# Two query/key buffers, first values in the weight ring, three weight loads from ScalarE's queue, a one-join decode and a new order, in a fused attention and two-MLP kernel

## Chip, cores and metric

The kernel runs on one core of a Trainium2 chip. The metric is the device time of one execution in microseconds. Before the change it was 1083.62 us, the median of three runs (1083.09 to 1084.38). The profiled execution took 1084.31 us, and the stretch that its trace covers, from the first to the last instruction, is 1082.5 us.

## What is computed

Chunked attention with memory slots, then a two-layer MLP with a rational activation, then a gated MLP. q, k and v are float32; all weights are float64.

```python
# attention: 4 batches, 8 heads, 768 positions, head dimension 64, chunks of 32 queries
for c in range(24):
    k_ctx = k[:, :, max(0, 32*c - 16) : min(768, 32*c + 40)]        # v_ctx the same
    k_full = concat([mem_k, k_ctx]); v_full = concat([mem_v, v_ctx]) # 8 memory rows first
    a = softmax(q_c @ k_full.T / 8)
    out[:, :, 32*c : 32*c + 32] = a @ v_full
x = attn_out as 3072 tokens x 512
h = x @ w_in                                        # 512 -> 2048
g = (a0 + a1*h + a2*h**2 + a3*h**3) / (1 + |b0|*|h| + |b1|*h**2 + 1e-6)
x = g @ w_out                                       # 2048 -> 512
y = (((x @ w1) * (x @ w2)) @ w3) @ w_out2           # 512 -> 1024 twice, gate, 1024 -> 1024 -> 512
```

## The kernel before

**Precision and decode.** A matmul with float32 accuracy is made of three passes (`mm3`, line 281; the `pe.matmul` is line 284): high part times high part, high times low, low times high. Each weight chunk, 128 x 512 values of float64, comes from HBM as 512 KB of raw 32-bit words into a ring of four tiles (`raw`). `decode` turns it into a high and a low part in seven steps: the load; `scale` (ScalarE, L242), which brings the upper word into float32's exponent range; `low` (L248 on ScalarE, L250 on VectorE), which takes the top three bits of the lower word; two joins (VectorE, L255 and L257); `high_part` (ScalarE, L265); `low_part` (L268, GpSimd, or VectorE for some chunks). `MODES` names, for each of the 32 chunks of the first MLP, where scaled values lie (PSUM bank "h" or "att", or in place) and which engine takes `low` (ScalarE for capital letters).

**Attention.** A unit u is 128 queries of all heads; there are 24, six in each batch. Its steps: `load_qk` (L299, four transfers of 64x4x160 words, and L302, four small ones for the memory keys, where the buffer is new to the batch), `load_v` (L308 to L311), scores `sc` on TensorE (L326), maximum, difference and sum on VectorE (L336, L339, L347), exponential on ScalarE (L343), normalization `e` (L357), transposition `at` on TensorE (L362), copies `aT` (ScalarE L371, VectorE L373), values `xo` on TensorE (L380), and the split into `xr`, high on ScalarE (L388), low on VectorE (L390). There is one buffer each for q/k, v and e.

**First MLP.** Tokens are in 8 blocks of 384, three units each; the 2048 hidden columns in 16 chunks f. Step n of `SEQ` is a block and an f: `gemm1` (h, 12 matmuls), the rational function (`rat_*`, ScalarE, VectorE, GpSimd), `gemm2` (acc, 12 matmuls), which trails by four steps. The first two blocks are interleaved by halves: block 0 with f 0 to 7 (here h0 to h7), block 1 with f 0 to 7 (h8 to h15), then f 8 to 15 of either (h16 to h31). So h8 needs units 3 to 5, and h16 the first weight chunk beyond the eighth. All 32 chunks are decoded beside these steps.

**Second MLP.** `ab` (L284) are the two gate inputs, `w3o` folds w3 and w_out2 into one matrix, `pr` are products of a seven-product scheme over half blocks.

**What sets the order.** Every operation is a `step` with a nominal time, the engines that can take it, what it follows, and the ring slots it takes. `order()` deals the steps out to the engines by earliest start and nominal time; the program is then written out in that order, and each engine runs its list strictly in that order. SP issues all transfers of this part from one list. Numbers such as `T0`, `UP`, `R`, `SI` or `DO` are only nominal times.

Of the kernel before, what the change touches and what calls it, by code (L numbers as in the profile page):

```python
# [41 lines left out]
SIGN = -2 ** 31  # L42

# [13 lines left out]
def attention_rational_mlp_gated_mlp(  # L57
# [18 lines left out]
    QBUF, VBUF, EBUF = 1, 1, 1  # L76
# [152 lines left out]
    def decode(t, src, dst, *ready, take=(), early=(), LOW=None, tag=None, byte=False):  # L229
# [5 lines left out]
        def load():  # L235
            r.append(raw("w64"))
            sp.dma_start(out=r[0], in_=src.bitcast(I32).rearrange("p (k t) -> p k t", t=2))
# [21 lines left out]

        def value():  # L260
            return b[0] if inps else r[0][:, :, 0].bitcast(F32)
# [31 lines left out]
    def load_qk(u):  # L293
        b, j = divmod(u, UPS)
        t = q_t[u % QBUF]
        for g in range(2):
            r, h = slice(g * D, (g + 1) * D), slice(g * HG, (g + 1) * HG)
            for s in range(NS):
                sp.dma_start(out=t[r, :, s, :QB + KW], in_=qkT[b, j * NS + s, :, h])  # L299
            if j < QBUF:  # L300
                for s in range(NS):
                    sp.dma_start(out=t[r, :, s, QB + KW:], in_=qkT[b, 0, :, h, QB:QB + NMEM])  # L302

    def load_v(u):
        b, j = divmod(u, UPS)
        t = v_t[u % VBUF]
        for s in range(NS):
            sp.dma_start(out=t[:CK, s], in_=vW[b, j * NS + s, :CK])  # L308
            sp.dma_start(out=t[CK:P - NMEM, s], in_=vW[b, j * NS + s, W1:])
            if j < VBUF:  # L310
                sp.dma_start(out=t[P - NMEM:, s], in_=vW[b, 0, :NMEM])  # L311
# [63 lines left out]
    def v_pe(u, tag):  # L375
        xo = st[u] = bank(tag, "xo")
        for s in range(NS):
            for h in range(H):
                i, g = divmod(h, 2)
                pe.matmul(xo[g * D:(g + 1) * D, i * UQ + s * QB:i * UQ + (s + 1) * QB], lhsT=v_t[u % VBUF][:, s, h],  # L380
                          rhs=aT[:, s, g * (H // 2) + i].rearrange("p c q -> p (c q)"), start=True, stop=True)
# [196 lines left out]
    H0 = 1.272  # L578


    MODES = "KNnhahkKkNNNNNNNHNmmHAaMAaaaANAn"
    HOW = {"n": (None, LOWA), "h": ("h", LOWA), "a": ("att", LOWA), "m": (None, two("d", 0, .602)), "k": ("h", two("d", 0, .64))}
# [14 lines left out]
    T0 = -8.139; UP = -3.210; A0 = -2.685; AS = 1.874  # L597
# [3 lines left out]
    SLACK = 0.4  # L601
    NORM = "pd"
# [3 lines left out]
    LEAD = 4  # L606
    LEAD2 = 9
    A1 = -2.388
    A2 = -2.780

    def loads(u, t):
        lq[u] = step(t - 3, {"dma": 2.65}, lambda: load_qk(u), *old(first, lq[u - 1]), take=("q",))
        lv[u] = step(t - 2, {"dma": 2.0}, lambda: load_v(u), *old(lv[u - 1]), take=("v",))
        return lq[u]
# [38 lines left out]
    R = (-1.427,0.216,0.543,0.964,1.286,6.975,-0.116,0.555,0.902,0.154,1.541,1.594,-0.009,-1.683)  # L653
    DI = -2.973
    DO = -3.438
    WI, WO = {}, {}
    SI = 0.893
    SO = 0.844
    DJ = -3.554
    DP = -3.457  # L660
    SJ = 0.944
# [40 lines left out]
    for k, (t, o, f) in enumerate(chunks):  # L702
        (WO if o else WI)[f] = decode(t, *((w_out[f], wB[:, f]) if o else (w_in[f], wA_slot(f))), tag=HOW[MODES[k].lower()][0],
                                      byte=MODES[k].isupper(), LOW=HOW[MODES[k].lower()][1])
# [20 lines left out]
    TG, TO, TM = 1.727, 0.363, -0.182  # L725
    TB = n1 + LAG - 0.1
    XB = 0
# [62 lines left out]
    for i in range(NF2):  # L790
        W3[i] = [decode(tO[i] + 0.5 * g + D3, w3T[i, :, g], w3_dst(i, g), sec, take=("w3",), early=[sec] if i < 2 else [O[i - 2]], LOW=LOWT[g % len(LOWT)], tag=TAGT[g % len(TAGT)], byte=BYTT[g % len(BYTT)]) for g in range(2)]
# [10 lines left out]
    LG2 = 3  # L802
# [13 lines left out]
    XT, XS, SL, SH, GT, OT = -6.742, -5.180, -1.545, 0.934, -2.825, -0.532  # L816
# [345 lines left out]
```

## Time and profile before

| | |
|---|---|
| time, median of three | 1083.62 us |
| profiled execution | 1084.31 us |
| its span | 1082.5 us |
| TensorE busy | 1040.6 us, 96% of the span |
| VectorE, ScalarE, GpSimd busy | 759.1, 671.6, 483.9 us |
| mean granted TensorE clock | 0.984 of full speed |

Busy time of TensorE contains slow stretches: the same twelve matmuls of 128x384 take about 2.1 us at full clock and about 4.1 us at half. So an idle gap can cost twice, once as a gap and once as the slow matmuls behind it. The program is a pipeline whose start has to be filled; the page's slices show TensorE at 90% or more from the fifth of the 40 slices on.

### The profile page before, as it was taken

The numbers are of one execution on the slowest core, as the hardware profiler recorded it, in microseconds if no ns is written. First come the engines' busy times: TensorE is split into PE (matmuls) and PEld (weight loads), VectorE is DVE, ScalarE is ACT, GpSimd is POOL, SyncE is SP. The second block draws the span as 40 slices with busy tenths as digits, with TensorE's granted clock in tenths as the row PEclk, the third lists the DMA queues.
The fourth block names the chain that finished last, engine by engine and source line by source line (L and its number), as shares of the span: only waits on it lengthen the run. The fifth ranks groups of instructions, "written<-read, shape, count | busy, mean of one in ns | idle before, by whom it ended". The sixth has DMA issues, their size and how long they took to land.

```text
span 1082.5 us, 20045 instructions
## 1 busy us (share of the span) xinstructions
PE 1040.6 (96%) x7632; PEld 985.5 (91%) x7632; DVE 759.1 (70%) x1326; ACT 671.6 (62%) x1290; POOL 483.9 (45%) x438
## 2 busy tenths in 40 slices
PE   2697999999999999999999999999999999999998
PEld 2587999999999999999999999988899999998997
DVE  4889999787777777777779987875485563663330
ACT  3687998677777777777779996644233252343222
POOL 1255675444434444444446776723133263344233
PEclk9688999999999999999999999999999999999999
DMA  8935363321131121211222335363324122312201
GB/s 211 255 116 153 109 199 89 101 90 48 44 92 49 44 74 45 73 44 53 65 97 78 117 99 166 126 185 126 118 102 155 57 86 69 107 40 78 69 20 59
DMA packets 65824, 105.71 MB, mean 98 GB/s; under 512 B 10624, under 2 KB 35328, under 8 KB 65728
## 3 DMA queue, kind: packets, MB, share of 16 engines
q1 hardware_dynamic: 65440, 104.36, 31.5%
q8 instruction: 60, 0.98, 0.4%
q14 instruction: 36, 0.29, 0.1%
q10 hardware_dynamic: 288, 0.07, 0.0%
HBM read 86.05 MB, written 18.35 MB: 96 GB/s over the span
## 4 chain that ended last, share of the span: by engine, by line
PE 84%; DVE 6%; ACT 6%; DMA 2%; SPq 1%; issue 1%; DVEq 0%; ACTq 0%
PE acc L284 32%; PE h L284 21%; PE pr L284 16%; PE ab L284 6%; PE w3o L284 4%; PE sc L326 2%; PE xo L380 2%; PE at L362 1%; DMA w<-in_w_out_dram 1%; DMA w<-in_w_in_dram 1%; DVE A L435 1%; ACT Q L413 1%; DVE h L439 1%; DVE A L443 1%; DVE A L422 1%
## 5 line engine op out<-in xcount | busy, mean ns | idle before, releaser
L284 PE MATMUL h<-xr,wA 128*128 128x384 f32 x1536 | 293.7, 341 | 3.7 <-ACT xr L388 2.3
L284 PE MATMUL acc<-gh,wB 128*128 128x384 f32 x1024 | 282.9, 339 | 0.0
L284 PEld LDWEIGHTS h<-xr,wA 128*128 128x128 f32 x1536 | 270.3, 190 | 8.3 <-ACT xr L388 2.7
L417 POOL TENSOR_TENSOR W<-W,Q 128x384 f32<-128x384 f32 x128 | 133.6, 1044 | 210.8 <-ACT Q L413 192.2
L284 PEld LDWEIGHTS acc<-gh,wB 128*128 128x128 f32 x1024 | 186.8, 188 | 1.2
L284 PE MATMUL acc<-gl,wB 128*128 128x384 f32 x512 | 172.3, 336 | 0.0
L452 POOL TENSOR_TENSOR gl<-A,gh 128x384 fp32r<-128x384 f32 x128 | 135.2, 1056 | 74.8 <-ACT gh L447 69.7
L284 PE MATMUL pr<-wB,wA 128*128 128x384 f32 x624 | 113.9, 335 | 0.0
L284 PEld LDWEIGHTS pr<-wB,wA 128*128 128x128 f32 x624 | 109.2, 188 | 1.3
L422 DVE TENSOR_TENSOR A<-A,h 128x384 f32<-128x384 f32 x128 | 70.4, 550 | 50.1 <-ACT A L405 49.6
L435 DVE SCALAR_TENSOR_TENSOR A<-A,cf,h 128x384 f32<-128x384 f32 x128 | 78.0, 609 | 33.2 <-ACT h L431 32.1
L284 PEld LDWEIGHTS acc<-gl,wB 128*128 128x128 f32 x512 | 96.1, 188 | 0.0
L405 ACT ACTIVATE W<-h 128x384 f32<-128x384 f32 x128 | 62.5, 489 | 49.2 <-PE h L284 47.2
L413 ACT ACTIVATE Q<-W,cf 128x384 f32<-128x384 f32 x128 | 90.6, 708 | 3.2
L284 PE MATMUL acc<-wB,gh 128*128 128x512 f32 x294 | 92.4, 395 | 0.0
L405 ACT ACTIVATE A<-h,cf 128x384 f32<-128x384 f32 x128 | 84.4, 659 | 0.0
L931 POOL TENSOR_TENSOR A<-A,Q 128x384 f32<-128x384 f32 x24 | 26.7, 1114 | 120.2 <-DVE A L931 117.1
L424 DVE SCALAR_TENSOR_TENSOR A<-A,cf,h 128x384 f32<-128x384 f32 x128 | 78.2, 611 | 3.2
L931 DVE TENSOR_TENSOR A<-pr,W 128x384 f32<-128x384 f32 x48 | 26.7, 556 | 74.5 <-PE pr L284 74.5
L431 ACT ACTIVATE h<-Q 128x384 f32<-128x384 f32 x128 | 63.3, 495 | 24.5 <-DVE A L424 21.4
L429 ACT ACTIVATE Q<-W 128x384 f32<-128x384 f32 x128 | 66.9, 523 | 18.2 <-POOL W L417 18.1
L443 DVE SCALAR_TENSOR_TENSOR A<-h,A 128x384 f32<-128x384 f32 x128 | 70.9, 554 | 2.8
(114 smaller groups left out, 1762.1 us busy)
## 6 DMA issues: line engine op xcount, KB each, us to landing
qk<-in_qkT_dram SPq DMA_DIRECT2D x96, 160.0 KB
w<-in_w_out_dram SPq DMA_DIRECT2D x24, 512.0 KB
sr<-sd SPq DMA_DIRECT2D x48, 256.0 KB
w<-in_w_in_dram SPq DMA_DIRECT2D x16, 512.0 KB
w<-in_w3T_dram SPq DMA_DIRECT2D x16, 512.0 KB
w<-in_w_dram SPq DMA_DIRECT2D x16, 512.0 KB
v<-in_vW_dram SPq DMA_DIRECT2D x48, 128.0 KB
out_dram<-oo SPq DMA_DIRECT2D x24, 256.0 KB
```

Of the source, the lines that this page charges most:

```text
L284: pe.matmul(out_, lhsT=wi(w, a), rhs=xi(x, c), start=first and i == 0, stop=last and i == 2, skip_group_check=more)
L405: act.activation(out=t, in_=hps[n][src], func=func, scale=scale, bias=bias)
L413: act.activation(out=t, in_=hps[n]["W"], func=AF.Identity, scale=cf[:, 5:6], bias=cf[:, 4:5])
L417: pool.tensor_tensor(out=W, in0=W, in1=Q, op=ALU.mult)
L422: dve.tensor_tensor(out=A, in0=A, in1=h, op=ALU.mult)
L424: dve.scalar_tensor_tensor(out=A, in0=A, scalar=cf[:, 1:2], in1=h, op0=ALU.add, op1=ALU.mult)
L429: act.activation(out=Q, in_=W, func=AF.Ln, bias=ONE)
L431: act.activation(out=h, in_=Q, func=AF.Exp, scale=-1.0)
L435: dve.scalar_tensor_tensor(out=A, in0=A, scalar=cf[:, 0:1], in1=r, op0=ALU.add, op1=ALU.mult)
L443: dve.scalar_tensor_tensor(out=A, in0=r, scalar=-2.0, in1=A, op0=ALU.add, op1=ALU.mult)
L452: eng.tensor_tensor(out=gl, in0=hps.pop(n)["A"], in1=gt[n].bitcast(F32), op=ALU.subtract)
L931: eng.tensor_tensor(out=t, in0=get(a), in1=get(b), op=ALU.add)
```

## The change

1. Two q/k buffers (`QBUF` 2), used in turn. The four small transfers of memory keys are gone; `mem_k`, a GpSimd copy of 128x64 words inside the tile, takes their place for the first two units of each batch.
2. The values of units 0 to 2 are loaded into tiles of the `raw` ring, not into the one v buffer, and each follows its q/k load. Unit 3 is then the first that uses the v buffer.
3. The first three weight chunks are issued by ScalarE's queue at the start of the program, not by SP.
4. `one`: in chunks whose scaled values lie in PSUM and whose `low` runs on ScalarE, `low` writes its three bits as a byte into the upper word, `keep` (VectorE, one source) clears the rest of that word but the sign, and one join does the rest.
5. New numbers for the nominal times, the modes and the places of some steps; `XB` 2 puts two more steps of gate inputs ahead of the `w3o` stage.

```diff
-    QBUF, VBUF, EBUF = 1, 1, 1
+    QBUF, VBUF, EBUF = 2, 1, 1
...
         def load(eng):
             r.append(raw("w64"))
-            sp.dma_start(out=r[0], ...)
+            eng.dma_start(out=r[0], ...)
...
             if eng is act:
                 top = r[0].bitcast(U8).rearrange("p k (t b) -> p k t b", b=4)[:, :, 0, 3]
-                act.activation(out=lo, in_=top, func=AF.Copy, scale=1.0 / 32, bias=-0.484375)
+                to = r[0].bitcast(U8).rearrange("p k (t b) -> p k t b", b=4)[:, :, 1, 0] if one else lo
+                act.activation(out=to, in_=top, func=AF.Copy, scale=1.0 / 32, bias=-0.484375)
...
+        def keep():
+            hi = r[0][:, :, 1]
+            dve.tensor_scalar(out=hi, in0=hi, scalar1=KEEP, scalar2=None, op0=ALU.bitwise_and)
+
+        def join1():
+            lo, hi, x = r[0][:, :, 0], r[0][:, :, 1], b[0].bitcast(I32)
+            dve.scalar_tensor_tensor(out=x if inps else lo, in0=x, scalar=3, in1=hi, op0=ALU.logical_shift_left, op1=ALU.bitwise_or)
...
+        if early_q:
+            a = step(-50, {"act": 0.37}, lambda: load(act), first, *early, take=("raw",))
+            a0, a = a, step(-50, {"dma": 2.0}, lambda: None, a)
...
+        if one:
+            c = step(t, {"act": 0.58}, lambda: low(act), a, s)
+            c = step(t, {"dve": 0.38}, keep, c, port=True)
+            c = step(t, {"dve": 0.64}, join1, c, frees=[a0] if inps else [s])
...
-            if j < QBUF:
-                for s in range(NS):
-                    sp.dma_start(out=t[r, :, s, QB + KW:], in_=qkT[b, 0, :, h, QB:QB + NMEM])
+    def mem_k(u):
+        t = q_t[u % QBUF]
+        pool.tensor_copy(out=t[:, :, :, QB + KW:], in_=t[:, :, :, QB:QB + NMEM])
...
-        t = v_t[u % VBUF]
+        t = vt[u] = raw32("v").rearrange("p (s h d) -> p s h d", s=NS, h=H) if u < UPB else v_t[u % VBUF]
...
-    MODES = "KNnhahkKkNNNNNNNHNmmHAaMAaaaANAn"
+    MODES = "KHnahhkKNkNNNNNNHNmmHAnMAaaaAANn"
...
+    QW = 3
-    LEAD = 4
-    LEAD2 = 9
+    LEAD = 3
+    LEAD2 = 7
...
+        return step(t - .1, {"pool": .2}, lambda: mem_k(u), lq[u], port=True) if mem else lq[u]
...
-    TG, TO, TM = 1.727, 0.363, -0.182
+    TG, TO, TM = 0.337, 0.404, -0.042
-    XB = 0
+    XB = 2
```

**How the order moves.** TensorE at the start of the program; sc are scores, at transpositions, xo value products, h the first matmuls of the MLP. Before:

```order
L326 MATMUL sc<-qk_83 32x64 x32
L362 MATMUL at<-idn,e_85 128x128 x4
L326 MATMUL sc<-qk_83 32x64 x32
L380 MATMUL xo<-aT,v_84 64x64 x16
L326 MATMUL sc<-qk_83 32x64 x32
L362 MATMUL at<-idn,e_85 128x128 x4
L380 MATMUL xo<-aT,v_84 64x64 x16
L362 MATMUL at<-idn,e_85 128x128 x4
L380 MATMUL xo<-aT,v_84 64x64 x16
L326 MATMUL sc<-qk_83 32x64 x32
L284 MATMUL h<-xr,wA 128x384 x36
```

TensorE at the same place, now:

```order
L348 MATMUL sc<-qk_83 32x64 x32
L348 MATMUL sc<-qk_84 32x64 x32
L348 MATMUL sc<-qk_83 32x64 x32
L384 MATMUL at<-idn,e_86 128x128 x4
L402 MATMUL xo<-aT,v 64x64 x16
L384 MATMUL at<-idn,e_86 128x128 x4
L402 MATMUL xo<-aT,v 64x64 x16
L384 MATMUL at<-idn,e_86 128x128 x4
L402 MATMUL xo<-aT,v 64x64 x16
L348 MATMUL sc<-qk_84 32x64 x32
L303 MATMUL h<-xr,wA 128x384 x24
L384 MATMUL at<-idn,e_86 128x128 x4
```

All three scores of the first block stand ahead of its first transposition, and two h steps instead of three ahead of unit 3's transposition.

ScalarE at the start; w_145 and w_147 are the first two weight chunks, e the exponentials of unit 0. Before:

```order
L591 ACTIVATE cf<-cf 128x2
L592 ACTIVATE cf<-cf 128x4
L242 ACTIVATE wx<-w_145 128x512
L343 ACTIVATE e_85<-e_85 128x512
L248 ACTIVATE w_145<-w_145 128x512
L242 ACTIVATE w_147<-w_147 128x512
```

ScalarE at the same place, now, with the chunks called w_103, w_105 and w_107:

```order
L613 ACTIVATE cf<-cf 128x2
L614 ACTIVATE cf<-cf 128x4
L238 DMA w_103<-in_w_in_dram 128x1024
L238 DMA w_105<-in_w_in_dram 128x1024
L238 DMA w_107<-in_w_in_dram 128x1024
L243 ACTIVATE wx<-w_103 128x512
L250 ACTIVATE w_103<-w_103 128x512
L243 ACTIVATE wx<-w_105 128x512
L250 ACTIVATE w_105<-w_105 128x512
L365 ACTIVATE e_86<-e_86 128x512
```

The exponential of unit 0 stood behind one step of the first chunk and now stands behind two steps of each of the first two.

ScalarE a little later: the cast of w_out chunk 9 into `wB` (w_1299 here) and what stands about it, row 196 of ScalarE's list. Before:

```order
L431 ACTIVATE h<-Q 128x384
L405 ACTIVATE A<-h,cf 128x384
L447 CAST gh<-A 128x384
L242 ACTIVATE wx<-w_1393 128x512
L248 ACTIVATE w_1393<-w_1393 128x512
L429 ACTIVATE Q<-W 128x384
L265 ACTIVATE wB<-w_1299 128x512
```

ScalarE around the same cast, now row 216 of its list; the chunk is called w_1489, and w_1464 is chunk 8:

```order
L451 ACTIVATE Q<-W 128x384
L275 ACTIVATE wB<-w_1464 128x512
L469 CAST gh<-A 128x384
L427 ACTIVATE A<-h,cf 128x384
L427 ACTIVATE W<-h 128x384
L435 ACTIVATE Q<-W,cf 128x384
L243 ACTIVATE wx<-w_1595 128x512
L275 ACTIVATE wB<-w_1489 128x512
```

The casts of w_out chunks 8 and 9 stood 60 and 80 rows behind unit 5's cast of `xr` (row 116 before, row 105 now) and now stand 105 and 111 rows behind it; with the copies that a row groups counted apart the distances are 61 and 81 before, 111 and 117 now. Between them now stand all remaining chunks of w_in, chunk 15 included.

On SP, the first weight load stood behind the q/k and values of unit 0; two chunks stood ahead of unit 1's q/k load, and three more between that and unit 2's. Now the first weight load on SP stands behind the q/k loads of units 0 to 4 and the values of units 0 to 3. Four chunk loads follow there, then unit 5's q/k load.

## Rows read from the trace of the kernel before

**Rows 1.** Stretches: start:end, length, busy us of each engine, granted clock, DMA share, GB/s.

```profile
core 0: us, PE busy (x) PEld busy (x) DVE busy (x) ACT busy (x) POOL busy (x), PEclk, DMA share, GB/s
0.00:44.28 44.28, 17.17 (x364) 14.07 (x365) 26.45 (x50) 18.60 (x33) 7.67 (x10) 0.77 0.91 232
44.28:94.61 50.33, 40.72 (x408) 37.67 (x405) 46.78 (x83) 42.61 (x83) 24.96 (x21) 0.91 0.55 155
94.61:103.32 8.71, 8.67 (x37) 8.27 (x37) 6.71 (x9) 5.60 (x11) 5.54 (x6) 0.73 0.52 151
103.32:175.00 71.68, 70.97 (x533) 69.41 (x536) 68.94 (x125) 70.46 (x142) 48.07 (x44) 1.00 0.41 131
175.00:1078.84 903.84, 903.04 (x6312) 856.12 (x6300) 610.27 (x1062) 533.75 (x1024) 397.63 (x360) 1.00 0.27 84
```

**Rows 2.** Waits of TensorE over the whole span: total us, times, longest.

```profile
PE sc L326 <- DMA qk<-in_qkT_dram: 10.4, 5, 4.3
PE at L362 <- DVE e L357: 9.5, 3, 8.6
PE xo L380 <- DMA v<-in_vW_dram: 5.5, 1, 5.5
```

**Rows 3.** Timeline of TensorE: start, us, operation, idle before it and its releaser.

```profile
17.56 1.11 PE L362 MATMUL at<-idn,e 128*128 128x128 f32 x4 [8.56 <-DVE e L357]
...
40.34 2.10 PE L380 MATMUL xo<-aT,v 128*64 128x64 f32 x32 [5.49 <-DMA v<-in_vW_dram]
...
57.91 4.09 PE L284 MATMUL h<-xr,wA 128*128 128x384 f32 x12
...
91.12 1.15 PE L380 MATMUL xo<-aT,v 128*64 128x64 f32 x32 [3.41 <-DVE aT L373]
94.61 8.87 PE L284 MATMUL h<-xr,wA 128*128 128x384 f32 x36 [2.34 <-ACT xr L388]
...
126.84 6.41 PE L284 MATMUL h<-xr,wA 128*128 128x384 f32 x36
```

**Rows 4.** Timeline of ScalarE, VectorE and SP in the first 100 us.

```profile
9.29 0.83 SPq L237 DMA_DIRECT2D w<-in_w_in_dram  x2
...
13.53 0.62 ACT L242 ACTIVATE wx<-w 128x512 f32<-128x512 f32 x1 [10.85 <-DMA w<-in_w_in_dram]
...
14.73 0.69 DVE L347 TENSOR_REDUCE sm<-e 128x8 f32<-128x512 f32 x1 [4.06 <-ACT e L343]
...
51.63 0.73 DVE L357 TENSOR_TENSOR e<-e,r 128x512 f32<-128x512 f32 x1
...
94.59 0.69 DVE L390 TENSOR_TENSOR xr<-xo,xr 128x512 fp32r<-128x512 f32 x1 [0.25 <-ACT xr L388]
```

**Rows 5.** VectorE's decode operations, first 110 us: count, busy, mean ns, idle before.

```profile
L255 DVE SCALAR_TENSOR_TENSOR wx<-wx,w 128x512 int32<-128x512 int32 x8 | 5.6, 694 | 2.6 <-ACT w L248 2.5
L250 DVE TENSOR_SCALAR w<-w 128x512 int32<-128x512 int32 x8 | 4.2, 530 | 0.0
```

**Rows 6.** Timelines of ScalarE, TensorE and GpSimd around w_out chunks 8 to 10.

```profile
93.98 0.57 ACT L388 CAST xr<-xo 128x512 fp32r<-128x512 f32 x1
...
138.48 0.66 ACT L265 ACTIVATE wB<-w 128x512 fp32r<-128x512 f32 x1
...
147.36 0.44 PE L284 MATMUL acc<-gh,wB 128*128 128x384 f32 x1
...
151.69 0.34 PE L284 MATMUL acc<-gh,wB 128*128 128x384 f32 x1
...
148.67 1.32 POOL L268 TENSOR_TENSOR wB<-w,wB 128x512 fp32r<-128x512 f32 x1 [1.75 <-ACT wB L265]
```

**Rows 7.** Timelines of TensorE and GpSimd in the w3o stage.

```profile
701.67 11.36 PE L284 MATMUL w3o<-wB,w 128*128 128x512 f32 x48
...
719.14 5.76 PE L284 MATMUL w3o<-wB,w 128*128 128x512 f32 x24
...
716.16 1.32 POOL L268 TENSOR_TENSOR w<-w,w 128x512 fp32r<-128x512 f32 x1 [0.46 <-ACT w L265]
```

More of the change, by code (lines that the diff above doesn't have):

```diff
@@ L222, in raw32, with decode @@
         return raw(name).rearrange("p k t -> p (k t)").bitcast(F32)
-    def decode(t, src, dst, *ready, take=(), early=(), LOW=None, tag=None, byte=False):
+    def decode(t, src, dst, *ready, take=(), early=(), LOW=None, tag=None, byte=False, one=False, early_q=False):
         r, d, b = [], [], []
@@ L233, in decode, with load @@
         inps = tag and "pool" not in LOW
-        def load():
+        def load(eng):
             r.append(raw("w64"))
-            sp.dma_start(out=r[0], in_=src.bitcast(I32).rearrange("p (k t) -> p k t", t=2))
+            eng.dma_start(out=r[0], in_=src.bitcast(I32).rearrange("p (k t) -> p k t", t=2))
         def scale():
@@ L604, in attention_rational_mlp_gated_mlp @@
     tcs = {}
-    LEAD = 4
-    LEAD2 = 9
-    A1 = -2.388
-    A2 = -2.780
+    LEAD = 3
+    LEAD2 = 7
+    A1 = -2.595
+    A2 = -2.583
     def loads(u, t):
-        lq[u] = step(t - 3, {"dma": 2.65}, lambda: load_qk(u), *old(first, lq[u - 1]), take=("q",))
-        lv[u] = step(t - 2, {"dma": 2.0}, lambda: load_v(u), *old(lv[u - 1]), take=("v",))
-        return lq[u]
+        mem = u < QBUF or u % UPS < QBUF
+        lq[u] = step(t - 3, {"dma": 2.7}, lambda: load_qk(u), *old(first, lq[u - 1]), take=("q",))
+        vm = u <= UPB or u % UPS < VBUF
+        lv[u] = step(t - 2, {"dma": 2.7 if vm else 2.1}, lambda: load_v(u), *old(lv[u - 1], lq[u] if u < UPB else None), take=("raw",) if u < UPB else ("v",))
+        return step(t - .1, {"pool": .2}, lambda: mem_k(u), lq[u], port=True) if mem else lq[u]
     old = lambda *a: [x for x in a if x]
@@ L650, in attend @@
         outs(u, t + 1.3 * k, k)
-    R = (-1.427,0.216,0.543,0.964,1.286,6.975,-0.116,0.555,0.902,0.154,1.541,1.594,-0.009,-1.683)
-    DI = -2.973
-    DO = -3.438
+    R = (-1.350,1.547,0.507,1.898,1.899,8.305,-0.920,0.209,1.296,0.774,0.422,0.707,0.378,-1.729)
+    DI = -2.774
+    DO = -3.013
     WI, WO = {}, {}
[L657 to L661, printed above, removed]
+    SI = 0.717
+    SO = 1.201
+    DJ = -2.740
+    DP = -2.000
+    SJ = 0.400
     chunks = sorted([(SI * f + DI if f < HF else SJ * (USE[f] - USE[HF]) + DJ + USE[HF], 0, f) for f in range(NF1)]
@@ L703, in attention_rational_mlp_gated_mlp @@
         (WO if o else WI)[f] = decode(t, *((w_out[f], wB[:, f]) if o else (w_in[f], wA_slot(f))), tag=HOW[MODES[k].lower()][0],
-                                      byte=MODES[k].isupper(), LOW=HOW[MODES[k].lower()][1])
+                                      byte=MODES[k].isupper(), LOW=HOW[MODES[k].lower()][1],
+                                      one=MODES[k].isupper() and HOW[MODES[k].lower()][0] is not None, early_q=k < QW)
     u = UPB
@@ L790, in attention_rational_mlp_gated_mlp @@
     for i in range(NF2):
-        W3[i] = [decode(tO[i] + 0.5 * g + D3, w3T[i, :, g], w3_dst(i, g), sec, take=("w3",), early=[sec] if i < 2 else [O[i - 2]], LOW=LOWT[g % len(LOWT)], tag=TAGT[g % len(TAGT)], byte=BYTT[g % len(BYTT)]) for g in range(2)]
+        W3[i] = [decode(tO[i] + 0.5 * g + D3, w3T[i, :, g], w3_dst(i, g), sec, take=("w3",), early=[sec] if i < 2 else [O[i - 2]], LOW=LOWT[g % len(LOWT)], tag=TAGT[g % len(TAGT)], byte=BYTT[g % len(BYTT)], one=BYTT[g % len(BYTT)]) for g in range(2)]
         t = tO[i]
```

40 lines of the change are left out of this document (22 added, 18 removed).

## The prediction

> **What bounds the kernel now.** I read the table of stretches first. From 103.32 us to 1078.84 TensorE is busy for 70.97 and 903.04 us of 71.68 and 903.84: 1.5 us are lost in 975 [rows 1]. TensorE's instructions are the same in kind and number with the change. So the time can fall only in the first 103 us, by more than is lost again later; and any stall put into the full part adds its length. In the first stretch TensorE works 17.17 of 44.28 us, while the DMA engines are 0.91 busy at 232 GB/s; in the second it works 40.72 of 50.33 us [rows 1]. The table of waits says for what: 10.4 us for queries and keys (`qk`), 9.5 for the normalized exponentials `e`, nearly all of it one wait of 8.6, and 5.5 for values `v` [rows 2]. TensorE's timeline gives their places: 8.56 us before the first transposition at 17.56, 5.49 before unit 2's value product at 40.34, then 3.41 at 91.12 and 2.34 at 94.61, where h8 waits for `xr` of unit 5 [rows 3].
>
> An idle gap costs a second time. Twelve h matmuls took 4.09 us at 57.91 and the 36 of h8 to h10 8.87 us at 94.61, against 6.41 for the same 36 at 126.84 [rows 3], where the granted clock is 1.00; around the slow ones it is 0.73 [rows 1]. So cold matmuls at h8 cost 8.87 - 6.41 = 2.5 us.
>
> Behind the start stands the second bound. From 103.32 to 175 ScalarE is busy 70.46 and VectorE 68.94 of 71.68 us [rows 1]. TensorE is just kept fed there by engines that have no slack of their own.
>
> **First transposition.** The exponential of unit 0 ran at once behind its maximum; the first chunk's scaling came at 13.53, and the sum behind the exponential at 14.73 [rows 4]. Now it stands on ScalarE behind the scaling and the three bits of two chunks. Ahead of the second chunk's last byte there are two q/k loads (4 x 64 x 4 x 160 words, 0.655 MB each) and two chunks (0.524 MB each), 2.36 MB. At 232 GB/s [rows 1] that is 10.2 us, about 10.9 with the issue. Two more steps of some 0.6 us and the exponential itself put the sum at about 12.8; before, the transposition came 17.56 - 14.73 = 2.8 us behind the sum, so it comes near 15.7, not at 17.56 [rows 3, 4]. Ends: 14.5, if VectorE alone sets it, and 17.9, if the second chunk lands as late as the first did (13.53).
>
> **Values, q/k and the first h.** With two q/k buffers, and v of units 0 to 2 in the ring, the 5.5 us for `v` and most of the 10.4 for `qk` [rows 2] have no cause left; next to be late is a weight. The first chunk that SP loads has 5 x 0.655 of q/k, 4 x 0.524 of v and three chunks ahead of it, with itself 7.47 MB: 32.2 us at 232 GB/s, 33 with the issue. Its scaling stands on ScalarE ahead of the cast of unit 2's `xr`, which h0 needs. So h0 begins in earnest near 35.7 (33.5 to 37.8), against 44.28, the end of the first stretch.
>
> The rows show that DMA time is what the start spends: SP issues its first weights only at 9.29 [rows 4], and yet the DMA share is 0.91 [rows 1]. The Trainium skill, "DMA: Bandwidth & Descriptors", section "Issuing engines are not separate DMA queues", says that transfers started by different engines run on the same 16 DMA engines and interleave, and that a second issuer saves only issue time. It speaks against the loads from ScalarE: by it they take bandwidth from unit 0's q/k. The trace of before has one issuer for these loads and can't show it; the rival "crowded" below prices it.
>
> **From h0 to h8.** Unit 3's normalization came at 51.63 [rows 4], 7.35 us behind h0; the same distance gives 43.1 to 43.3. From there to the low part of unit 5's `xr` at 94.59 [rows 4] VectorE had 68 instructions in 42.96 us, 0.632 each. Now there are 71: 44.9 us, to 88.2. Among those, chunks with `one` put a one-source `keep` for a join: a like instruction takes 530 ns, the join 694 [rows 5], 0.16 us saved per chunk (29 chunks, of which 9 here; below zero where the one-source form is held up, as far as the 0.69 of the join). Four of them give 0.6: I take 87.6 (86.3 to 90). Then h8 starts at 88.3, 6.3 us earlier than 94.61. Against that the second part of block 0's fifth step, 2.1 us, isn't done before h8 any more; for it the 2.5 us of cold matmuls should go, since TensorE has work up to h8. The lead is 6.3 - 2.1 + 2.5 = 6.7 us. The small copies `mem_k` on GpSimd wait for q/k, with parts of g queued behind them; GpSimd was busy 24.96 of 50.33 us [rows 1], so I price them at nothing, and at up to 0.5 us if q/k is late.
>
> **What the decodes give back.** The lead is kept only if the weights come 6.7 us earlier as well. ScalarE's cast of w_out chunk 9 stood 81 instructions behind unit 5's `xr` cast and now stands 117 behind it; for chunk 8 it is 61 and 111. Before, the 81 took from 93.98 to 138.48 [rows 6], 44.5 us, of which 3.1 were idle between 94.61 and 103.32 (8.71 - 5.60 [rows 1]), and about 1.5 spread out. With what each kind of instruction takes there, start to start, the 111 come to 54.6 us and the 117 to 57.7. From a cast of unit 5's high part at about 87.0, chunk 8's cast begins at 141.6 without idle time. Its cast (0.66) and low part on GpSimd (1.32 [rows 6]) end at 143.6. Its first matmul was at 147.36 [rows 6]: the lead there can't exceed 147.4 - 143.6 = 3.7 us. For chunk 9 it is 151.69 - (87.0 + 57.7 + 2.0) = 4.9. Each us that ScalarE idles comes off; with all of the old idle time (4.6) the lead would be -0.9. VectorE's rows give much the same: 88 instructions to chunk 8's join. Since h8 no longer comes late and cold, I take 0.7 us of idle time: TensorE waits at 140 to 155 us for `wB`, gives back 3.7 of the 6.7, and **3.0 us** are left (0.7 to 4.6).
>
> **The second MLP.** The `w3o` steps are reordered; 20 of the 29 `one` chunks are there. Before, a decode ended at 716.16 + 1.32 = 717.5 for a step at 719.14, which ran from 713.03 on without it (701.67 + 11.36) [rows 7]: 1.7 us of slack. The products between the steps stay, so I price it at nothing. From 175 us VectorE is 0.68 and ScalarE 0.59 busy [rows 1], so fewer joins there give nothing to the end.
>
> **Rivals.**
> - *Clipped* (forecast): a lead of about 6.7 us at h8, most of it given back by 155 us. 1084.31 - 3.0 = 1081.3 for the profiled execution; it is 0.7 above the median, so 1080.6 for the median (1079.0 to 1082.9). For it: ScalarE at 70.46 of 71.68. Chance 0.55.
> - *Kept*: ScalarE and VectorE come to unit 5 earlier than I count, and the decodes keep up: 5 to 7 us, about 1077. Against it: 36 to 50 more instructions stand ahead of the casts. 0.17.
> - *Paced*: VectorE sets unit 5 at about 90 and ScalarE keeps its idle time; the lead is -0.9 to 1 us: 1083.6. 0.07.
> - *Crowded*: the first chunks take bandwidth from q/k of units 0 and 1, the exponential waits for the second chunk, the transposition comes at 17.9 and h0 at 37.8. The lead at h8 is 3.8, and ScalarE, late by the same 2.9 (unit 5 at 90), clips it to 0.8 (0 to 2.5): 1082.8. The rule above is its ground; the row of 13.53 gives its bound. 0.08.
> - *Slower*: each `w3o` step now has its decode later than its slot. The decode can start only when the step two places ahead has freed its buffer, and in the new order a half product stands ahead of the third `w3o` step that stood elsewhere. With the 1.7 us of slack used up and another 1.1 us missing, six steps (all but the first two) cost 6.6, against 3.0 gained: 1087.2. It decides from 0.5 us late each on. Against it: slack of 1.7 [rows 7], two more steps of `ab` ahead of the stage. 0.13.
>
> **How the numbers follow.** The measurement tells 0.2%, 2.2 us, from no change, so faster means below 1081.45 and slower above 1085.8. *Clipped* is split 0.44 faster and 0.11 the same, *kept* is faster, *paced* the same, *crowded* 0.03 and 0.05. Faster 0.64, same 0.23, slower 0.13. The range leaves out the lower half of *kept* and most of *slower*: 1076.5 to 1084.5. The likeliest time is 1080.6.
>
> **What would show it.** In the profile after: the first transposition near 15.7 us, no wait for `v`, h0 at 35 to 36, h8 near 88.3 and its 36 matmuls in about 6.4 us. Then, new, waits of TensorE for `wB` between 140 and 155 us, some 3 to 4 us together, and none in the `w3o` stage near 700 to 770 us. TensorE's waits for `wB` missing with h8 at 88 would make it *kept*; h8 beyond 91 *paced* or *crowded*, which the first transposition tells apart; waits for the `w` tiles of `w3o` *slower*. The prediction is wrong if the time is above 1084.5, or if the gain comes from behind 175 us.

## The result

The changed kernel takes 1092.96 us (median of four runs, 1091.21 to 1094.75), the kernel before 1084.0 in the same measurement: a ratio of 1.0079 with a 95% interval of 1.0056 to 1.0103, 9 us slower. The forecast was 1080.6 and faster. The profiled execution took 1094.75 us, its span is 1092.9, TensorE is busy 1042.2 us (1040.6 before): of the 10.4 us by which the span grew, 8.8 are idle time of TensorE.

The stretches of the changed kernel, with the columns of [rows 1]; the last two of [rows 1] are cut at 135 and 180 us here:

```profile
core 0: us, PE busy (x) PEld busy (x) DVE busy (x) ACT busy (x) POOL busy (x), PEclk, DMA share, GB/s
0.00:44.28 44.28, 14.55 (x333) 11.94 (x337) 20.68 (x37) 14.73 (x23) 4.16 (x9) 0.86 0.81 206
44.28:94.61 50.33, 41.51 (x433) 38.90 (x424) 47.27 (x85) 42.31 (x79) 23.69 (x22) 0.85 0.56 168
94.61:135.00 40.39, 38.19 (x216) 36.90 (x215) 33.93 (x63) 39.97 (x78) 26.77 (x24) 1.00 0.39 129
135.00:180.00 45.00, 40.83 (x310) 37.96 (x308) 40.45 (x78) 43.28 (x84) 29.19 (x26) 1.00 0.47 147
180.00:1078.00 898.00, 895.69 (x6310) 849.49 (x6309) 599.18 (x1067) 548.06 (x1024) 393.20 (x363) 1.00 0.27 84
```

The kernel before in the last three of these stretches, same columns:

```profile
94.61:135.00 40.39, 40.23 (x216) 39.25 (x216) 36.79 (x63) 36.92 (x73) 25.74 (x24) 0.94 0.38 118
135.00:180.00 45.00, 44.21 (x394) 42.82 (x393) 43.85 (x82) 42.84 (x87) 29.45 (x27) 1.00 0.47 145
180.00:1078.00 898.00, 897.42 (x6254) 851.40 (x6255) 605.27 (x1052) 529.42 (x1016) 396.06 (x358) 1.00 0.27 84
```

Against 17.17 us in the first stretch [rows 1] TensorE now works 14.55: instead of gaining, the start has lost 2.6 us of work, and 0.8 us of it come back in the second stretch (41.51 against 40.72). From 94.61 to 135 it loses 2.0 us more than before, where ScalarE is now busy 39.97 of 40.39; from 135 to 180 3.4 us; behind 180, 1.7 us. TensorE's waits, which answer to [rows 2]:

```profile
PE sc L348 <- DMA qk<-in_qkT_dram: 12.8, 3, 5.1
PE xo L402 <- DVE aT L395: 8.3, 5, 2.0
PE sc L348 <- issue: 6.6, 1, 6.6
PE at L384 <- DVE e L379: 6.5, 4, 4.1
PE h L303 <- DVE A L465: 4.5, 6, 1.6
PE sc L348 <- POOL qk L322: 4.4, 2, 4.0
PE at L384 <- DVE w L268: 1.3, 1, 1.3
```

The wait for `v` of [rows 2] is gone, but q/k takes 12.8 and not 10.4, GpSimd's copy of the memory keys 4.4, and a wait of 6.6 has come that the profile lays to no engine. The six waits of h for the end of the rational function (`A`, L465), 4.5 us, were two of 0.4 us together in the kernel before.

**The start, row by row.** TensorE of the changed kernel, which answers to [rows 3]:

```profile
9.78 0.64 PE L348 MATMUL sc<-qk 64*32 64x64 f32 x14 [5.08 <-DMA qk<-in_qkT_dram]
10.82 1.70 PE L348 MATMUL sc<-qk 64*32 64x64 f32 x50 [0.40 <-POOL qk L322]
...
20.60 3.21 PE L348 MATMUL sc<-qk 64*32 64x64 f32 x112 [4.01 <-POOL qk L322]
23.74 1.11 PE L384 MATMUL at<-idn,e 128*128 128x128 f32 x4
...
43.44 1.93 PE L348 MATMUL sc<-qk 64*32 64x64 f32 x64 [6.59 <-issue]
45.31 6.26 PE L303 MATMUL h<-xr,wA 128*128 128x384 f32 x24
...
95.01 2.35 PE L303 MATMUL h<-xr,wA 128*128 128x384 f32 x12
```

Here h0 is the row at 45.31 and h8 the row at 95.01 (94.61 before [rows 3]). Who was ahead: GpSimd (two rows), ScalarE (four), VectorE (three) and SP (two) of the changed kernel:

```profile
19.08 1.29 POOL L278 TENSOR_TENSOR wA<-w,wA 128x512 fp32r<-128x512 f32 x1 [8.31 <-DMA v<-in_vW_dram]
20.31 0.24 POOL L322 COPY qk<-qk 128x64 f32<-128x64 f32 x1
...
10.02 1.35 ACT L250 ACTIVATE w<-w 128x512 uint8<-128x512 uint8 x1
15.00 0.62 ACT L243 ACTIVATE wx<-w 128x512 f32<-128x512 f32 x1 [3.63 <-DMA w<-in_w_in_dram]
...
41.24 0.65 ACT L243 ACTIVATE wx<-w 128x512 f32<-128x512 f32 x1 [7.14 <-DMA w<-in_w_in_dram]
41.81 0.58 ACT L410 CAST xr<-xo 128x512 fp32r<-128x512 f32 x1
...
18.10 0.68 DVE L369 TENSOR_REDUCE sm<-e 128x8 f32<-128x512 f32 x1
...
20.66 0.69 DVE L379 TENSOR_TENSOR e<-e,r 128x512 f32<-128x512 f32 x1
...
42.66 0.69 DVE L259 SCALAR_TENSOR_TENSOR w<-w,wx 128x512 int32<-128x512 int32 x1
...
0.74 13.58 SPq L318 DMA_DIRECT2D qk<-in_qkT_dram  x12
...
36.67 1.50 SPq L238 DMA_DIRECT2D w<-in_w_in_dram  x3
```

Unit 0's scores end at 12.5 us and not at 9.0, since three weight chunks now move beside its q/k. Its exponential stands on ScalarE behind the second chunk, whose scaling waited 3.63 us for its load and began at 15.00; so the sum came at 18.10 and the normalized `e` was ready at 21.4. Unit 1's scores wait until 20.60: the copy of its memory keys (20.31) stands on GpSimd behind the second chunk's low part, whose cast is late. The first transposition stands behind all three scores and comes at 23.74, 2.4 us after its own `e`. Unit 2's cast of `xr` (41.81) stands on ScalarE behind the fourth chunk's scaling, which waits 7.14 us for a load that SP issued only at 36.67. The same late load makes the wait of 6.59 without an engine. By the source, the fourth chunk's scaled values and the scores of unit 3 share the one PSUM bank "att"; the chunk's second join, which frees it, ends at 43.35 on VectorE, and the scores start at 43.44. h0 stands behind them on TensorE.

**The byte write.** ScalarE's `low` in its two forms, the whole run of the changed kernel and of the kernel before (count, busy us, mean ns):

```profile
L250 ACT ACTIVATE w<-w 128x512 uint8<-128x512 uint8 x29 | 39.9, 1374 | 1.3
L250 ACT ACTIVATE w<-w 128x512 int32<-128x512 uint8 x10 | 6.7, 665 | 0.0
```

```profile
L248 ACT ACTIVATE w<-w 128x512 int32<-128x512 uint8 x39 | 26.1, 671 | 0.0
```

Writing a byte in place of a word doubles the instruction, by 0.70 us: 29 of them are 20.5 us of ScalarE's time, nine of them before 175 us.

### The profile page after: what moved, and what is told of

The parts are those of the page before. It is cut to its first block, busy times and chain, and to the rows that moved or that the text cites. A ratio compares the mean times of both kernels' runs of the same rounds, so it can differ in the third digit from the quotient of the medians.

```text
span 1092.9 us, 20047 instructions
## 1 busy us (share of the span) xinstructions
PE 1042.2 (95%) x7632; PEld 984.0 (90%) x7632; DVE 741.5 (68%) x1327; ACT 691.1 (63%) x1289; POOL 479.8 (44%) x446
## 4 chain that ended last, share of the span: by engine, by line
PE 70%; ACT 13%; DVE 8%; DMA 5%; issue 2%; SPq 1%; POOL 1%; ACTq 0%; DVEq 0%; POOLq 0%
PE acc L303 27%; PE h L303 17%; PE pr L303 16%; PE ab L303 3%; PE w3o L303 3%; PE sc L348 2%; ACT Q L435 2%; PE xo L402 2%; DMA w<-in_w_in_dram 2%; ACT w L250 1%; ACT A L427 1%; ACT W L427 1%; ACT h L453 1%; DMA w<-in_w3T_dram 1%; ACT gh L469 1%
## 5 line engine op out<-in xcount | busy, mean ns | idle before, releaser
L439 POOL TENSOR_TENSOR W<-W,Q 128x384 f32<-128x384 f32 x128 | 131.3, 1027 | 235.6 <-ACT Q L435 215.7
L474 POOL TENSOR_TENSOR gl<-A,gh 128x384 fp32r<-128x384 f32 x128 | 132.1, 1033 | 43.9 <-ACT gh L469 22.3
L427 ACT ACTIVATE W<-h 128x384 f32<-128x384 f32 x128 | 62.5, 488 | 51.9 <-PE h L303 50.3
L465 DVE SCALAR_TENSOR_TENSOR A<-h,A 128x384 f32<-128x384 f32 x128 | 70.9, 555 | 2.9
```

The lines of the kernel that those rows point to most:

```text
L427: act.activation(out=t, in_=hps[n][src], func=func, scale=scale, bias=bias)
L439: pool.tensor_tensor(out=W, in0=W, in1=Q, op=ALU.mult)
L465: dve.scalar_tensor_tensor(out=A, in0=r, scalar=-2.0, in1=A, op0=ALU.add, op1=ALU.mult)
L474: eng.tensor_tensor(out=gl, in0=hps.pop(n)["A"], in1=gt[n].bitcast(F32), op=ALU.subtract)
```

## The experiments

All ratios are to the kernel before, measured beside each run. The steps in the table are matmul steps (twelve matmuls of h or acc), counted on TensorE's timeline; a time there is good to about 1 us. By the records of the single matmuls the three steps end at 101.4, 135.3 and 172.3 us in the kernel before, and at 103.2, 138.4 and 180.3 in the changed one.

| kernel | median us | ratio, 95% interval | step 16 | step 32 | step 48 |
|---|---|---|---|---|---|
| before | 1082.8 to 1084.0 | 1 | 100.6 | 134.5 | 171.1 |
| changed | 1092.96 | 1.0079 (1.0056 to 1.0103) | 103.0 | 139.4 | 179.9 |
| word_low | 1088.36 | 1.0049 (1.0033 to 1.0066) | 100.7 | 134.8 | 176.8 |
| old_in_slots | 1088.23 | 1.0054 (1.0039 to 1.0069) | 102.3 | 137.7 | 178.5 |
| before_skip | 1080.33 | 0.9970 (0.9960 to 0.9981) | 98.1 | 132.2 | 168.7 |
| start_fix | 1096.85 | 1.0128 (1.0106 to 1.0151) | 104.3 | 140.4 | 182.7 |
| one_off | 1091.63 | 1.0070 (1.0048 to 1.0092) | 103.4 | 137.9 | 179.9 |
| before_one | 1093.91 | 1.0094 (1.0076 to 1.0112) | 100.9 | 134.6 | 177.2 |
| before_newpos | 1090.89 | 1.0076 (1.0061 to 1.0091) | 101.3 | 135.1 | 179.3 |
| word_low_oldpos | 1094.32 | 1.0119 (1.0096 to 1.0141) | 100.3 | 134.3 | 181.0 |
| before_pool3 | 1086.61 | 1.0027 (1.0013 to 1.0042) | 97.7 | 132.3 | 173.4 |
| early1_pool3 | 1085.35 | 1.0014 (0.9998 to 1.0031) | 97.0 | 131.7 | 172.4 |

**1. The byte write, at a fixed order.** All engines keep their instructions in the changed kernel's order.

```diff
-                to = r[0].bitcast(U8)....[:, :, 1, 0] if one else lo
+                to = lo
```

> The changed kernel, same order, but in the 29 one-join decodes the three bits are written as a whole word into the lower word and not as a byte into the upper one (so keep and the join work on the upper word's own three bits: that part of the decode is left out). The trace after shows the byte form at 1374 ns and the word form at 665. Theory A (the byte write is what starves TensorE behind 100 us): 9 x 0.71 = 6.4 us less ScalarE work in the first MLP, TensorE's idle time between 94.61 and 175 us falls from 6.4 us by 4 or more, the w3o stage loses its 2 us, time 1086 to 1088. Theory B (the late start and the new order do it, ScalarE only waits elsewhere): 1091 to 1093.

It came to 1088.36 us, 4.6 under the changed kernel; by the ratios, 0.3%, 3.3 us. Theory A's range was missed by 0.4 us. The waits in and around the `w3o` stage are gone: between 690 and 790 us TensorE is busy 100.00 us and was 98.01. From 94.61 to 180 us 1.4 of the lost 5.4 us come back, the rest not:

```profile
94.61:135.00 40.39, 38.74 (x220) 37.67 (x219) 35.90 (x67) 39.53 (x80) 27.42 (x25) 1.00 0.43 138
135.00:180.00 45.00, 41.65 (x367) 39.63 (x367) 40.98 (x78) 41.03 (x82) 28.10 (x26) 0.96 0.44 134
```

The true undoing, with both old joins in the slots of `keep` and the one join:

```diff
-            dve.tensor_scalar(out=hi, in0=hi, scalar1=KEEP, ...)
+            join(0)
...
-            dve.scalar_tensor_tensor(out=x if inps else lo, in0=x, scalar=3, in1=hi, ...)
+            join(1)
```

> The changed kernel's order, instruction for instruction, with the old decode in the same slots: word write, then the two old joins where keep and the one join stand. This is the whole undoing of the one-join decode at a fixed order. Theory A (the byte write is the whole of its cost, the saved joins worth 0.16 us each): 1088 to 1090, at most 1.5 above word_low's 1088.4. Theory B (the saved joins matter): 1091 or more, as one_off.

1088.23 us: level with word_low. So the saved joins are worth nothing that can be measured, and the one-join decode costs 3 to 5 us, by the byte. The size is rough: the interval of either run overlaps that of the changed kernel, but the two runs agree, and in both traces TensorE's 2.0 us between 690 and 790 us come back. Two thirds of the loss (a ratio of 1.0054) stay. Dealt out anew without it:

```diff
-  one=MODES[k].isupper() and HOW[...][0] is not None, early_q=k < QW
+  one=False, early_q=k < QW
```

> The changed kernel with no one-join decode at all (both MLPs decode as before, with two joins), dealt out anew by the planner with the new numbers. Theory A (the byte write is the larger part of the loss, the start the rest): as with the word form, 1087 to 1089, since VectorE's saved joins (0.16 us each) aren't worth more than 1 us. Theory B (the saved joins carried the plan): 1090 or more.

1091.63 us, in B's range and 2.6 over A's, but not for B's reason, since old_in_slots shows the saved joins to be worth nothing. By the ratios it is 1.7 us above the same decode in the changed kernel's slots; the intervals overlap, so this run alone doesn't show that the newly dealt order is worse. The next one does.

```diff
-            c = step(t, {"act": 0.58}, lambda: low(act), a, s)
+            c = step(t, {"act": 1.25}, lambda: low(act), a, s)
```

> The changed kernel with the planner told 1.25 us in place of 0.58 for the byte write of the one-join decode; the work is the same. Theory A (the cost itself): ScalarE still has 6 us more to do before 175 us, 1090 to 1094. Theory B (only the plan was wrong): the loss of the byte form goes, 1087 to 1089.

1108.59 us, 16 us more than the changed kernel for telling the planner nearly the true price; the work is the same, so it is only how the planner dealt it out. Neither theory had that. In the kernel before, the one-join decode alone, with `keep` and `join1` as in the change:

```diff
+  one=MODES[k].isupper() and HOW[MODES[k].lower()][0] is not None
```

> The kernel before with the one-join decode alone, in the 27 chunks or so that its own modes make eligible; everything else, the numbers included, stays. Theory A: byte writes cost ScalarE 0.71 us each, 7 of them in the first MLP where it has 1.2 us of slack in 71.7: waits of TensorE appear before 175 us, 1086 to 1090. Theory B: VectorE's saved joins make up for it: 1083 to 1084.

1093.91 us, 4 over A's range. Its start is level with before up to the 32nd step (134.6 against 134.5), and 6 us are lost by the 48th. It was also dealt out anew, so the byte's share of it isn't told apart.

**2. The start.**

```diff
+            for s in range(NS if u < QBUF or j < QBUF else 0): sp.dma_start(out=t[r, :, s, QB + KW:], ...)
...
-        return step(t - .1, {"pool": .2}, lambda: mem_k(u), ...)
+        return step(t - .1, {"pool": .2}, lambda: None, ...)
```

> The changed kernel with the memory keys of the first two units of each batch loaded by four small transfers again, in place of the GpSimd copy; ScalarE, VectorE and TensorE keep their order. Theory A: unit 1's scores waited 4.0 us for a copy queued behind a decode step, so the first transposition comes at about 20 and not at 23.7, but h0 is set by the weight that SP loads behind its queue, so the total moves by 0 to 1.5 us: 1091 to 1093. Theory B (the copy sets the start): h0 3 to 4 us earlier, 1088 to 1089.

1094.84 us (ratio 1.0104): TensorE's wait for GpSimd went and the one for q/k grew from 12.8 to 16.5, the first transposition stayed at 23.98. With its 4.4 us for GpSimd the changed kernel waits 17.2 us, against 16.5 here, and the times aren't told apart (1.0089 to 1.0119 against 1.0056 to 1.0103): the small transfers of 64x4x8 words gain nothing over the copies that they replace. So the copy's place was no net loss against the transfers.

```diff
-    QW = 3
+    QW = 0
```

> The changed kernel with the first three weight loads on SP again, dealt into the list by the planner (behind the values of units 0 to 3). Theory A (the weights crowd unit 0's q/k): unit 0's scores end at 9 us and not at 12.5, the first transposition comes before 18; but the weights land later, and h0 comes no earlier than 43: 1090 to 1096. Theory B (early weights are what gets h0 going): h0 at 48 or later, 1095 to 1100.

1106.50 us (1.0209), over every range. TensorE's start there:

```profile
7.38 1.70 PE L348 MATMUL sc<-qk 64*32 64x64 f32 x50 [0.51 <-POOL qk L322]
...
13.87 1.12 PE L384 MATMUL at<-idn,e 128*128 128x128 f32 x4 [1.88 <-DVE e L379]
...
39.15 1.01 PE L303 MATMUL h<-xr,wA 128*128 128x384 f32 x2 [11.66 <-ACT wA L275]
```

Without the early weights unit 0's scores end at 9 us and its transposition comes at 13.87, 10 us earlier than in the changed kernel, in another order too. So the weights do crowd q/k. But the weights themselves then hold h0 (11.66 us for `wA`), and later h steps wait another 12.5 us for the rational function. Next, two things that stood ahead of the chain were taken away, and the one-join decode with them (`one=False`, as in one_off, which is the kernel to compare with):

```diff
-    MODES = "KHnahh...
+    MODES = "KKnahh...
...
-    lv[u] = step(t - 2, {"dma": 2.7 if vm else 2.1}, ...)
+    lv[u] = step(t - 2, {"dma": (4.5 if u < UPB else 2.7) if vm else 2.1}, ...)
```

> The same without the one-join decode, and two edits at the start: the second chunk's low part on VectorE (nothing stands ahead of the memory-key copy on GpSimd), and the loads of values of units 0 to 2 counted by the planner at 4.5 us and not 2.7, nearer to what SP's issues took, so that unit 2's cast of xr stands ahead of the fourth chunk's scaling on ScalarE and VectorE. Theory A (what stands ahead of the chain on in-order engines holds the start): first transposition near 19 to 20, unit 3's scores near 33 to 36 and not 43.4, h0 at 36 to 38, total 1080 to 1085. Theory B (the start is bound by bytes): h0 within 2 us of 45, 1087 to 1089.

```profile
36.80 7.60 PE L303 MATMUL h<-xr,wA 128*128 128x384 f32 x36
46.01 0.63 PE L384 MATMUL at<-idn,e 128*128 128x128 f32 x4 [1.60 <-DVE e L379]
49.28 1.88 PE L402 MATMUL xo<-aT,v 128*64 128x64 f32 x32 [2.65 <-DVE aT L395]
52.91 1.93 PE L348 MATMUL sc<-qk 64*32 64x64 f32 x64 [1.76 <-DVE xr L412]
```

h0 came at 36.80, as theory A said, 8 us earlier than in one_off (44.83) and 8.5 than in the changed kernel, and the time rose from one_off's 1091.63 to 1096.85 us (1.0128). The early h0 brought nothing: h8 comes at 94.88 (one_off 99.57, changed 95.01, before 94.61), and the 16th step, at 103.4 us in one_off and 103.0 in the changed kernel, at 104.3. The rows show TensorE waiting for VectorE unit after unit. VectorE isn't full there: it is busy 44.7 of the 50.3 us from 44.28 to 94.61, less than the 46.78 of the kernel before [rows 1]. Which steps make the way from h0 to h8 58 us long and not 50 isn't shown; the order is a newly dealt one here too. This run upsets the forecast's sum more than any other.

The kernel before with two q/k buffers alone, its memory keys by transfer:

```diff
-    QBUF, VBUF, EBUF = 1, 1, 1
+    QBUF, VBUF, EBUF = 2, 1, 1
```

> The kernel before with two q/k buffers alone, memory keys by small transfers, its own numbers. Theory A: two buffers put all three scores first and move q/k bytes ahead of the weights on SP; the first transposition waits for the third score and the weights come later: slower, 1085 to 1092. Theory B: the 10.4 us of waits for q/k go: 1076 to 1081.

1094.97 us (1.0106), 3 over A's range; theory B falls. All three scores stand ahead of the first transposition (21.47 us), as in the changed kernel, and h0 comes at 44.8. h8 comes only at 102.02, 7.4 us later than before: here most of the loss is made ahead of h8, unlike in the changed kernel. Early weights in the kernel before:

```diff
+    early_q=k < 1        (in the second: k < 2)
```

> The kernel before with the first weight chunk's load alone on ScalarE's queue (issued near 2.4 us and not at 9.3), its own numbers and modes, dealt out anew. Theory A (early weights fill the idle start of ScalarE and VectorE; half a megabyte delays the first q/k by under 2 us): 1080 to 1084. Theory B (they crowd the q/k of unit 0, as in the changed kernel, where its scores ended at 12.5 and not at 9.0): the first transposition at 19 or later, 1085 to 1088.

> The same with two chunks on ScalarE's queue. Theory A: 1080 to 1084; theory B: more of the same delay, 1086 to 1091.

1083.29 us (0.9998, 0.9987 to 1.0009) and 1085.64 (1.0016, 1.0003 to 1.0029). One early chunk does no harm and no good, two cost a little. Unit 0's scores end at 9.0 us without an early chunk, at 11.0 with one and at 13.25 with two: the crowding grows with each. Theory A's range holds the first; the second lies just under B's.

**3. Is decode work on VectorE the bound?** The second join, the sign, is left out in the last 24 chunks of the first MLP, in the changed kernel without the one-join decode and in the kernel before.

```diff
-            else:
+            elif not skip:
                 dve.scalar_tensor_tensor(out=x if inps else lo, in0=hi, scalar=SIGN, ...)
```

> The changed kernel without the one-join decode, and without the second join (the sign) in the last 24 of the 32 chunks of the first MLP: that part of the decode is left out, 24 VectorE instructions of 0.68 to 0.86 us, 16 to 20 us, in the same order otherwise. Theory A (decode work that the later weights push out of the idle start into the stretch where VectorE and ScalarE are full is what costs the time): the waits of TensorE for the rational function's end (6.3 us) shrink and the time falls by 4 to 8 us from 1091.6, to 1084 to 1088. Theory B (the start alone, transfers and order): within 2 us of 1091.6.

> The kernel before with the same 24 second joins left out. Theory A: behind 103 us TensorE never waits there, so only the chain to h8 at 94.6 can gain, with about 8 of the 24 ahead of it: 1 to 5 us, 1079 to 1083. If it gains as much as the changed kernel does, VectorE's pace bounds both alike and the later weights aren't the difference.

1089.53 us (1.0062), 2.1 less than one_off and between the theories, and 1080.33 (0.9970), 3.4 less than before. The same 24 instructions are gone in either, and the changed one gains no more. So VectorE's joins alone aren't what its order lacks. In one_off_skip VectorE only waits more for ScalarE: 14.7 us from 44 to 175 us for the steps of the rational function, 7.5 in one_off. With the word form and 16 joins less (`skip=k >= 16`):

> word_low with the last join left out in the last 16 chunks of the first MLP (that part of the decode is missing): 16 VectorE instructions of 0.7 to 0.85 us, some 12 us, off the stretch from 75 to 165 us. Theory A (VectorE's and ScalarE's decode work in that stretch is the bound): 1084 to 1086.5. Theory B (ScalarE's list alone, which keeps all its decode steps, sets the pace): 1087 to 1089.

1086.61 us (1.0040): 1.8 under word_low, 1.0 by the ratios, within the intervals and at the line between the theories. Decode work on VectorE is at most a part of what is short there.

**4. Where the rest goes.** Word_low is level with the kernel before at the 32nd step and 5.7 us behind at the 48th. Only the three numbers that place the second half of the chunks, put into the kernel before, whose start stays as it was:

```diff
-    DJ = -3.554
-    DP = -3.457
-    SJ = 0.944
+    DJ = -2.740
+    DP = -2.000
+    SJ = 0.400
```

> The kernel before with the three new numbers for the second half of the chunks alone (SJ 0.400, DJ -2.740, DP -2.000); its first 118 instructions on ScalarE stay, and the cast of w_out chunk 8 moves from row 176 to 207, chunk 9 from 196 to 214. Theory A (the later casts cost the 5 us): 1087 to 1090, level with before at the 32nd step (134.5 us) and 4 to 6 us behind at the 48th. Theory B (they fill slack): within 1.5 us of 1083.7.

```profile
94.61:135.00 40.39, 39.35 (x212) 38.49 (x213) 35.52 (x62) 35.26 (x71) 24.24 (x23) 0.93 0.35 112
135.00:180.00 45.00, 39.09 (x361) 37.09 (x360) 42.22 (x78) 42.94 (x86) 29.45 (x27) 1.00 0.52 157
```

1090.89 us (1.0076), a little over A's range. With an untouched start, up to the 32nd step 0.6 us behind, it loses 8 us by the 48th: TensorE works 39.09 of 45.00 us and not 44.21, while ScalarE and VectorE are about as busy as before. So the position of these decode steps alone can cost the whole loss. (The numbers move all steps of these chunks, not the casts only.) The converse, word_low with the three old numbers:

> The changed kernel with word writes in the one-join decodes (their three bits then come from the wrong word, as in word_low) and the old three numbers for the second half. Theory A: 1083 to 1085.5, 3 to 5 us under word_low's 1088.4. Theory B (the start or the other numbers cost the rest): 1087 to 1090.

1094.32 us (1.0119): theory A falls in its simple form. The old three numbers in the changed order are worse still than the new ones, again between the 32nd and the 48th step (134.3, 181.0). What costs there isn't one set of numbers. One sign of how is in VectorE's waits for ScalarE's steps of the rational function, from 100 to 180 us in the changed kernel:

```profile
DVE A L457 <- ACT h L453: 4.9, 6, 1.3
DVE A L444 <- ACT A L427: 2.9, 4, 1.3
```

In the kernel before, the same two waits:

```profile
DVE A L422 <- ACT A L405: 3.0, 4, 1.0
DVE A L435 <- ACT h L431: 0.4, 1, 0.4
```

They are 3.4 us before, 6.2 in word_low and in before_newpos, 7.8 in the changed kernel and 10.1 in word_low_oldpos. They are a sign and no measure, as before_skip waits longer there than before and is faster. That casts and rational steps don't mesh on ScalarE's list is the reading that fits; no run isolates it.

**5. A better version?** Three low parts from VectorE to GpSimd in the kernel before, and the same with one early chunk:

```diff
-    MODES = "KNnhahkKkNN...
+    MODES = "KNnhahhHhNN...
```

> The kernel before with the low parts of chunks 6 to 8 (in order of loading) on GpSimd and not on VectorE, else its own numbers. Three VectorE instructions of 0.69 us leave the stretch from 38 to 50 us. Theory A (VectorE's list up to unit 5 sets h8): h8 at 92.5 to 93.5 and not 94.6, 1081 to 1082.5. Theory B (any newly dealt order disturbs the stretch behind 100 us more than that): 1084 to 1090.

> The same with the first chunk's load on ScalarE's queue as well, which by itself changed nothing (1083.29 against 1083.69). Theory A: 1080.5 to 1082.5; theory B: 1084 to 1090.

1086.61 and 1085.35 us: theory B's range in both, though the second can't be told from no change (0.9998 to 1.0031). The table shows how: at the 32nd step they lead by 2.2 and 2.8 us, as meant, and at the 48th they are 2.3 and 1.3 us behind. A lead won in the start is eaten between 135 and 175 us, and a little more than eaten. Before_skip, which leads by as much but has less to decode behind the start too, keeps it. No version here that does the whole work beats the kernel before.

## Why the prediction was wrong, step by step

The sum failed at two terms. The lead of 6.7 us at h8 was none (95.01 against 94.61), and behind h8 not 3.7 us were given back but about 10, since the profiled span grew by 10.4.

- **Full after 103 us, gain only ahead of it:** right of the kernel before. That a stall put into the full part adds its length was right as well, and became the result.
- **First transposition, 15.7 us (14.5 to 17.9):** 23.74. Most of the 8 us is the second chunk: its scaling was to follow a landing near 10.9 and began at 15.00, later even than the 13.53 that gave the range its end, and the sum came at 18.10, not 12.8. The step let only 2.36 MB move ahead of it, at 232 GB/s. The trace gives 163 GB/s up to 9.36 us and 251 from there to 15.00, an estimated 2.9 MB. The last 2.4 us are the other two scores, which the new order shows ahead of it, and which the step left out, with the copy of unit 1's memory keys behind a decode step on GpSimd, priced at 0 to 0.5 us; that wait was 4.0. The rule of the Trainium skill ("DMA: Bandwidth & Descriptors", "Issuing engines are not separate DMA queues"), that transfers of different issuers run on the same 16 DMA engines and interleave, had the better side, and the traces agree: unit 0's scores ended 3.5 us later with the weights beside them, and at 9 us again in sp_weights.
- **Values and q/k:** the wait for `v` did go. q/k rose from 10.4 to 12.8.
- **h0 at 35.7 (33.5 to 37.8):** 45.31. The cause was named, the first chunk that SP loads, though it held h0 through unit 3's scores, which need the bank of that chunk's scaled values, and not through unit 2's `xr` (the join ends at 43.35, the scores start at 43.44). The time of the load was mis-sized: 7.47 MB were to have landed in 33 us at 232 GB/s and took 41.2, 181 GB/s. The rate of a stretch in which weights, of 512 KB each, keep the queues full was used for one in which SP issues eighteen pieces of values of up to 128 KB one behind the other (14.99 to 27.3 us, at 163 GB/s and a DMA share of 0.70). Start_fix shows 36.80 to be possible.
- **h8 at 88.3, a lead of 6.7:** 95.0, none. That h8 follows h0 at a fixed distance fails by start_fix as well: with h0 8.5 us earlier than in the changed kernel, h8 came at 94.88 and the 16th step 1.3 us later.
- **29 chunks with one join:** only VectorE's side was priced (0.16 us each, right: `keep` takes 512 ns, the join 686). The changed output of `low`, in the diff, was taken for free. It is the largest price that the sum left out: 0.70 us each on the engine that the forecast itself called full, 3 to 5 us in all.
- **Decodes give back, between 140 and 155 us:** that later decode steps cost time there holds (before_newpos), and the place is nearly right: most is lost from 135 to 180 us. The size is wrong, as the lead was bounded by -0.9 us, and without the byte write it falls to about -5. The wait is wrong too: only 0.5 us are waits for `wB`; for `A`, the end of the rational function, TensorE waits 4.5. That the rational steps come late because they share two full lists with the decode steps is a reading, not shown by itself.
- **The second MLP, nothing:** 2.0 us, between 690 and 790 us, gone with the byte write. Only 0.5 of them is a wait for a decoded `w`; the others are for results of ScalarE and VectorE there. With the old decode in the same order (old_in_slots) TensorE is busy 99.98 of the 100 us, so the reordering alone was rightly priced at nothing.
- **Rivals:** *slower* had the sign (0.13); of its waits for `w` only 0.5 us came, and the loss lies elsewhere. *Crowded* was half of what happened in the start. No rival had a lead of zero at h8 together with a give-back; *paced* came nearest, with a net lead of -0.9 to 1 us.

What stays open: which steps in the stretch from 135 to 180 us must stand where. Before_newpos shows that positions alone can cost 7 to 8 us, word_low_oldpos that the old positions don't repair the new order. The share of the start's own lateness in the 5 us that are left isn't separated from the order, and the values in the ring, the new modes and the other new numbers were not run by themselves.

## What to carry to other kernels

Price every operand of a changed instruction, its output type and stride too, and on the engine that has least slack first. Where two engines are full behind the start, a faster start is worth only as much as they can follow: measure a lead at a landmark behind the full stretch, not at its entry. And an order that was dealt out for full engines is a part of the kernel: three edits that changed nothing but nominal times (planned_byte, before_newpos, word_low_oldpos against word_low) cost 6 to 16 us through how the steps were dealt out, so compare an edit at a fixed order first.

## What the hardware showed that was not expected

- A ScalarE instruction of 128x512 that writes single bytes at a stride of eight took 1374 ns, the same one writing 32-bit words at the same stride 665 to 671.
- Eight small transfers of 64x4x8 words at the start were no better than two GpSimd copies of the same data (0.24 us each there): TensorE waited 16.5 us for q/k, against 12.8 for q/k and 4.4 for the copies.
